# A second block of filter rows turned by DMA instead of TensorE, in a kernel whose order is a searched list

## The chip, the cores and the metric

The kernel runs on one core of one Trainium2 chip. The metric is the device time of one execution in microseconds (us). Three executions of the kernel before took 339.56, 339.56 and 339.36 us, median 339.56. A core has engines that run side by side, each one strictly through its own list of instructions: TensorE (PE, matrix multiplies into PSUM), VectorE (DVE), ScalarE (ACT), GpSimd (POOL) and SyncE (SP), whose list holds nearly all DMA issues. An engine stops at an instruction whose operand has not been signalled yet, and everything behind it in its list stops too.

## The reference, cut to what matters

Two kinds of layer alternate, twice each, on a sequence of 2048 rows of 512 columns in bfloat16:

```
def A(q, k, v, shift_k, ssm_k, ssm_D):            # long convolution
    kv = (4-tap causal filter of k along the rows, one tap set per column) * v
    y  = irfft(rfft(kv, 4096) * rfft(ssm_k, 4096))[:2048]     # along the rows, per column
    y  = y + kv * ssm_D
    return q * y
def B(x, w_gate, w_up, w_down):                   # gated MLP, 512 -> 1792 -> 512
    return (silu(x @ w_gate) * (x @ w_up)) @ w_down
x = A_q
x = x + A(layernorm(x), A_k, A_v, A_shift_k, A_ssm_k, A_ssm_D)
x = x + B(layernorm(x), B_w_gate, B_w_up, B_w_down)
(the same two lines once more)
```

In both A layers k, v, the taps and the filter are the same, so the convolution's result is computed once and used twice. The filter `ssm_k` is called h below; it lies in memory as 512 columns by 2048 rows, that is, turned against the layout in which the transform needs it.

## The kernel before, in words

**Blocks.** The 2048 rows are cut into four blocks of 512 rows. A block lies in SBUF as 128 partitions by four interleaved rows (`R = 4`) by 512 columns. The convolution works by blocks: `X[i]` is the spectrum of block i of kv, `H[b]` that of block b of h, `G[b]` joins `H[b]` and `H[b-1]`, and block k of the result is the inverse transform of the sum of `X[i]*G[j]` over i + j = k. The transforms are matmuls with tables of sines and cosines (`fwd`, `inv`) followed by additions on DVE. The MLP works on units of 256 rows (layer, block, half). For a unit, TensorE multiplies with `wg_sb` and `wu_sb` into PSUM (tile `pf`), ACT evicts both products, DVE multiplies them, and TensorE multiplies with `wd_sb` (tile `pd`). Some units take the down product by a seven-product scheme (`STRASSEN`, function `seven`), which needs sums of blocks of the down weights; `weight_sums` makes them once.

**How h is turned.** `load_h` (L428 and following, one DMA of 512 KB a block) brings block b into `hn` as columns by rows. `spectrum_h` then makes `hs`, rows by columns, in one of two ways, chosen by `H_DMA`. `transpose_h` uses TensorE: 16 transposes of 128x128 (L567) into two PSUM tiles, each evicted by one ACT copy of 128x1024 (L577). `transpose_h_dma` uses four ACT copies of 128x512 that put the rows apart (`hr`, L681) and then four SBUF-to-SBUF DMA transposes on SP's queue, one per interleaved row (L685). `forward4` follows in both cases: for each of the four rows of `hs`, two matmuls of 512 columns, each into a PSUM bank of its own that ACT evicts (L509). In the kernel before, blocks 0 and 1 of h are turned on TensorE and blocks 2 and 3 by DMA. Block 0's spectrum is evicted as the string `EVE` says, one letter for each of its eight banks (A for ACT L509, D for DVE L512).

**The order.** The program first records every operation in a `Plan`, with its engine, a cost that the author estimated, and its operands. The list `ORDER` holds one rank for each recorded operation; sorting by rank gives the order in which each engine's instructions are issued. `walk` lays the sorted operations on a time line by the estimated costs; that only decides which slot of a ring of buffers a tile takes and where idle matmuls (`wm`) warm TensorE at the start. So the order around the change is a fixed list; nothing is decided while the kernel runs.

**Rings.** A ring is a set of equal buffers: `s8` has eleven, `h`, `k`, `hs` have one each, `pf` (PSUM) four. An operation that writes a new tile into a ring waits until the readers of the tile that had the slot are done.

**The opening stage.** The first MLP unit cannot start before the first block of the convolution is done: spectra of block 0 of h and kv (L509, L548), their products on DVE (L732, L736), the inverse transform (L879), the layer norm (L898, L889, L950), and a transpose on TensorE (`ptz`, L1008) evicted into `zT` (L1011, L1013). TensorE fills the gaps of that chain with the convolution's block 1: turning h (L567), its forward matmuls (`ps<-hs,fwd`, L400), and the tap filter of k (`ps<-dg,kTb`, L400, 16 matmuls of 128 columns for each of four rows).

**SP's queue in the opening stage**, in its order: the loads of h, k, v, q, block 1 of h and v, the gate weights, two DMA transposes for `inv`, one for block 1 of k, the up weights, the down weights in two parts, block 1 of q, block 2 of h, block 2 of k.

Of the kernel before, what the change touches and what calls it, by code (L numbers as in the profile page):

```python
# [9 lines left out]
P = 128  # L10
# [9 lines left out]
H_DMA = lambda b: b in {2, 3}  # L20
# [13 lines left out]
LH0 = 4.0  # L34
# [7 lines left out]
EVE = "ADADAAAA"  # L42
# [80 lines left out]

PASSES, WARM, FETCH, PHASE, TOOK = 4, 33, 256, 173, 1.1

NS = 8
BLOCKS = [("C", 0, 1), ("C", 1, 1), ("C", 2, 1), ("C", 3, 1),
# [198 lines left out]
def kernel(  # L328
# [58 lines left out]
    def whole(name, shape, dtype=BF16, parts=1):  # L387
        return new("one", name, shape, dtype, parts)
# [631 lines left out]
    ws = {}  # L1020
# [498 lines left out]
```

## Time and profile before

| what | value |
|---|---|
| median of three runs | 339.56 us |
| the profiled execution, its own time | 340.1 us |
| its span (first to last instruction) | 338.3 us |
| PE busy | 333.9 us, 99% |
| DVE busy | 299.8 us, 89% |
| ACT busy | 265.0 us, 78% |
| POOL busy | 34.5 us, 10% |
| granted TensorE clock | 1.0 |

A row of a group reads: line, engine, operation, output and inputs, how many, then busy time and mean duration. Matmuls overlap in the pipeline, so the mean duration of one (379 ns for 512 columns) is longer than its step from one to the next; the chain that ended last gives the step. A row of SP's timeline is the time in which SP issues a transfer, not the time in which data move; the "to landing" rows count from the start of the issue until the transfer is signalled as done. A releaser is inferred from semaphores.

### The profile page before, as it was taken

What the parts mean: (1) busy time and instruction counts of PE and PEld (TensorE: products, weight loads), DVE (VectorE), ACT (ScalarE), POOL (GpSimd) and SP (SyncE); (2) the same over time, 40 slices, a digit from 0 to 9 for tenths busy, and PEclk for the clock granted to TensorE, in tenths of its full rate; (3) what the DMA queues carried; (4) which work ended last, traced back from release to release, by engine and by line L of the source; (5) the groups of instructions that cost most, each with busy time, mean ns of one, the idle gap of its engine ahead of it and who ended that gap; (6) DMA issues with size and microseconds to landing.
All of it is one profiled execution on the core that took longest, in us unless ns stands there. A gap on an engine that the chain in (4) does not pass through costs nothing.

```text
span 338.3 us, 5940 instructions
## 1 busy us (share of the span) xinstructions
PE 333.9 (99%) x2172; PEld 205.7 (61%) x2172; DVE 299.8 (89%) x508; ACT 265.0 (78%) x543; POOL 34.5 (10%) x48
## 2 busy tenths in 40 slices
PE   9999999999999999999999999999999999999996
PEld 8665865645454564745444564644546587867884
DVE  7899999999779997999999999989997967977465
ACT  6989999999987477989999886989765555566473
POOL 4010011003100000132030000101200010100000
PEclk9999999999999999999999999999999999999999
DMA  7999501443355336381333263510504230203201
GB/s 266 341 290 365 75 0 33 84 107 90 64 125 93 81 79 155 62 159 32 62 48 67 57 107 116 105 34 16 96 16 96 56 85 2 48 17 78 64 3 62
DMA packets 77992, 31.59 MB, mean 93 GB/s; under 512 B 69765, under 2 KB 75786, under 8 KB 77962
## 3 DMA queue, kind: packets, MB, share of 16 engines
q1 hardware_dynamic: 77808, 31.13, 39.8%
q8 instruction: 17, 0.28, 0.3%
q14 instruction: 13, 0.11, 0.1%
q10 hardware_dynamic: 154, 0.07, 0.1%
HBM read 12.33 MB, written 2.10 MB: 43 GB/s over the span
## 4 chain that ended last, share of the span: by engine, by line
PE 87%; ACT 7%; DVE 5%; issue 1%; POOL 0%; DVEq 0%; POOLq 0%
PE pf L400 50%; PE pd L1200 17%; PE ps L1075 7%; PE ps L400 7%; PE ps L548 2%; ACT jk L922 2%; PE wm L1485 1%; PE ps L879 1%; ACT sg L1113 1%; ACT hr L1114 1%; ACT X L509 1%; PE pt L567 1%; DVE t L746 1%; DVE m L630 1%; DVE Z L750 1%; DVE t L742 1%
## 5 line engine op out<-in xcount | busy, mean ns | idle before, releaser
L400 PEld LDWEIGHTS <-zT 128*128 128x128 bf16 x528 | 51.5, 98 | 59.4 <-DMA zT<-z 0.9
L400 PE MATMUL pf<-wu_sb,zT 128*128 128x512 bf16 x264 | 65.0, 379 | 0.0
L400 PE MATMUL pf<-wg_sb,zT 128*128 128x512 bf16 x264 | 64.9, 379 | 0.0
L1200 PE MATMUL pd<-wd_sb,sg 128*128 128x512 bf16 x200 | 49.4, 379 | 0.0
L1113 ACT ACTIVATE sg<-pf 128x512 bf16<-128x512 f32 x66 | 38.7, 604 | 11.4 <-PE pf L400 10.3
L400 PE MATMUL pf<-zT,wg_sb 128*128 128x256 bf16 x368 | 46.7, 273 | 0.0
L1114 ACT CAST hr<-pf 128x512 bf16<-128x512 f32 x66 | 38.2, 591 | 9.6 <-PE pf L400 9.0
L400 PE MATMUL pf<-zT,wu_sb 128*128 128x256 bf16 x368 | 45.4, 273 | 0.2 <-ACT zT L1013 0.2
L742 DVE TENSOR_TENSOR t<-X,G 128x4096 bf16<-128x4096 bf16 x18 | 41.0, 2280 | 0.1
L400 PEld LDWEIGHTS <-wg_sb 128*128 128x128 bf16 x368 | 36.0, 98 | 8.0
L400 PEld LDWEIGHTS <-wu_sb 128*128 128x128 bf16 x368 | 36.0, 98 | 7.1 <-issue 0.5
L1173 ACT ACTIVATE sg<-pf 128x512 bf16<-128x512 f32 x46 | 27.5, 606 | 10.9 <-PE pf L400 9.7
L1177 ACT CAST ht<-pf 128x512 bf16<-128x512 f32 x46 | 27.3, 599 | 10.8 <-PE pf L400 10.4
L889 POOL TENSOR_TENSOR rstd<-mv,nhalf 128x2 f32<-128x2 f32 x20 | 18.5, 928 | 160.3 <-DVE mv L899 160.3
L1200 PEld LDWEIGHTS <-sg 128*128 128x128 bf16 x200 | 19.6, 98 | 21.5
L1200 PE MATMUL pd<-wd_sb,ht 128*128 128x512 bf16 (+1 forms) x126 | 29.1, 369 | 0.0
L898 DVE BATCH_NORM_STATS2 bst<-xc 128x6 f32<-128x512 bf16 x40 | 26.4, 682 | 0.5
L1180 DVE TENSOR_TENSOR ht<-ht,sg 128x512 bf16<-128x512 bf16 (+1 forms) x31 | 16.7, 546 | 9.5 <-ACT sg L1173 6.2
L889 POOL TENSOR_TENSOR rstd<-ve,nhalf 128x2 f32<-128x2 f32 x12 | 12.4, 1032 | 112.3 <-ACT ve L926 112.3
L1120 DVE TENSOR_TENSOR hr<-hr,sg 128x1024 bf16<-128x1024 bf16 x27 | 18.4, 681 | 4.3 <-ACT hr L1114 2.3
L509 ACT ACTIVATE X<-ps 128x512 bf16<-128x512 f32 x32 | 18.8, 611 | 2.2 <-DVE Z L746 1.1
L1200 PEld LDWEIGHTS <-ht 128*128 128x128 bf16 x126 | 12.3, 98 | 12.8 <-ACT z L945 0.3
(143 smaller groups left out, 525.7 us busy)
## 6 DMA issues: line engine op xcount, KB each, us to landing
hn<-in_A_ssm_k_dram SPq DMA_DIRECT2D x4, 512.0 KB, 4.0
vt<-in_A_v_dram SPq DMA_DIRECT2D x4, 512.0 KB, 6.0
xc<-in_A_q_dram SPq DMA_DIRECT2D x4, 512.0 KB, 5.3
out_dram<-xc SPq DMA_DIRECT2D x15, 128.0 KB, 1.8
wg_sb<-in_B_w_gate_dram SPq DMA_DIRECT2D x1, 1792.0 KB
wu_sb<-in_B_w_up_dram SPq DMA_DIRECT2D x1, 1792.0 KB, 7.9
wd_sb<-in_B_w_down_dram SPq DMA_DIRECT2D x1, 1280.0 KB, 13.2
sg<-hr SPq DMA_TRANSPOSE x66, 2.4
```

The lines of the kernel that those rows point to most:

```text
L400: nc.tensor.matmul(o, lhsT=lhsT, rhs=rhs, start=(n == 0), stop=(n == len(terms) - 1))
L509: add("ACT", act(D), lambda: nc.scalar.activation(out=view(), in_=ps.t[:], func=ACT.Copy, scale=scale), r=[ps], w=[(buf, keys)], conv=conv)
L742: dve(8 * D, lambda t=t, part=part: nc.vector.tensor_mul(out=t.t[:], in0=x.t[:, :, part:part + 1, :].to_broadcast((P, R, 2, D)), in1=g.t[: ...
L889: add("POOL", cost, lambda: nc.gpsimd.tensor_tensor(out=rstd.t[:], in0=var(), in1=nhalf.t[:].to_broadcast((P, n)), op=ALU.pow), r=reads + ...
L898: add("DVE", 0.6, lambda st=st, i=i: nc.vector.bn_stats(out=st.t[:, 0:6], in_=xs[c].t[:, i, :]), r=[(xs[c], (i,))], w=[st])
L1075: nc.tensor.matmul(bank.t[:, half_ * C:(half_ + 1) * C], lhsT=lhsT(i), rhs=rhs(i), start=(first and i == 0 and half_ == 0), stop=(last and ...
L1113: add("ACT", act(D), lambda ps=ps, dst=dst, o=o, which=which: nc.scalar.activation(out=rows(dst, o), in_=ps.t[:], func=ACT.Silu) if which ...
L1114: out=rows(dst, o), in_=ps.t[:], func=ACT.Silu) if which == "g" else nc.scalar.copy(out=rows(dst, o), in_=ps.t[:]),
L1120: dve(n * W, lambda: nc.vector.tensor_mul(out=hr.t[:], in0=hr.t[:], in1=sg.t[:]), [sg], [hr], due=(unit, k / pairs, 0.0, "h"))
L1173: add("ACT", act(D), lambda ps=ps, o=o, sg=sg: nc.scalar.activation(out=sg.t[:, o:o + 2, :], in_=ps.t[:], func=ACT.Silu), r=[ps], w=[(sg, ...
L1177: add("ACT", act(D), lambda ps=ps, o=o, ht=ht: nc.scalar.copy(out=ht.t[:, o:o + 2, :], in_=ps.t[:]), r=[ps], w=[(ht, (o // 2,))], due=(uni ...
L1200: nc.tensor.matmul((pds[o] if not cs.start else pds[HP]).t[:, cs], lhsT=ht.tiles(q, o), rhs=wt["d"].t[:, ft, cs], start=(ft == std0 and no ...
```

## The change

Five edits:

1. `H_DMA` takes block 1 in: its h is turned by `transpose_h_dma` too.
2. The second letter of `EVE` goes from D to A: one eviction of block 0's spectrum of h moves from DVE (L512) to ACT (L509).
3. `weight_sums` writes five tiles of one size into the rings `h`, `k`, `hs`, `dg` and `s8`, where it wrote three tiles into `s8`; the diagonal tap tables `dg` get a ring of their own, so that their buffer can be used again. `seven` reads the tiles under the new names. Two of the five additions take even and odd rows of the weights instead of the lower and upper half.
4. Two numbers of the planner change: the estimated landing of block 0's h (`LH0`, 4.0 to 3.85), and a longer cost of TensorE's operations in the first 5.4 us (`RAMP`).
5. `ORDER` is another list, with 1725 ranks where there were 1721 (four operations fewer on TensorE and ACT, eight more on ACT and SP).

```
-H_DMA = lambda b: b in {2, 3}
+H_DMA = lambda b: b in {1, 2, 3}
...
-LH0 = 4.0
+LH0 = 3.85
...
-EVE = "ADADAAAA"
+EVE = "AAADAAAA"
...
 ORDER = [
-    1, 64, 179, 187, 2, 5, 0, 11, 15, 3, 4, 8, 14, 34, 36, 9, 7, 10, 6, 13, 19, 18, 17, 16, 20, 25, 27, 45, 51, 41, 47, 48, 31, 55, 33, 42, 32, 39,
...
+    4, 29, 43, 46, 3, 6, 5, 14, 21, 2, 11, 0, 36, 37, 38, 8, 9, 7, 10, 12, 22, 13, 16, 19, 20, 31, 33, 32, 44, 39, 52, 54, 28, 41, 27, 50, 30, 61, 40,
...
-PASSES, WARM, FETCH, PHASE, TOOK = 4, 33, 256, 173, 1.1
+PASSES, WARM, FETCH, PHASE, TOOK, RAMP = 4, 33, 256, 173, 1.1, 5.4
...
             o.end = o.start + o.cost
+            if o.eng == "PE" and o.start < RAMP:
+                o.end += 0.48 * min(1.92 * o.cost, RAMP - o.start)
...
-    dg = whole("dg", [P, KD, KS, P], parts=KD * KS)
+    dg = new("dg", "dg", [P, KD, KS, P], parts=KD * KS)
...
-        a = ws["14"] = new("s8", "wsa", [P, 2, NF // 2, C], parts=2)
-        b = ws["3"] = new("s8", "wsb", [P, NF // 2, C])
-        c = ws["67"] = new("s8", "wsc", [P, NF, C])
...
+        a0, a1 = (new(ring, "wsa", [P, NF // 2, C]) for ring in ("h", "k"))
+        b = new("hs", "wsb", [P, NF // 2, C])
+        c0, c1 = (new(ring, "wsc", [P, NF // 2, C]) for ring in ("dg", "s8"))
+        ws.update({"1": a0, "4": a1, "3": b, "6": c0, "7": c1})
+        for out, x0, x1, op in ((a0, lambda: ev(lo), lambda: od(hi), ALU.add), (b, lambda: ev(hi), lambda: od(hi), ALU.subtract),
+                                (a1, lambda: od(lo), lambda: ev(lo), ALU.subtract), (c0, lambda: ev(lo), lambda: ev(hi), ALU.add),
+                                (c1, lambda: od(lo), lambda: od(hi), ALU.add)):
+            dve(NF // 2 * C, lambda out=out, x0=x0, x1=x1, op=op: nc.vector.tensor_tensor(out=out.t[:], in0=x0(), in1=x1(), op=op),
+                [wd], [out])
```

What the new list does to the opening stage is read from the instruction lists of the two kernels. SP's queue, from the tap-filtered block 1 of k on:

```
before                              after
block 1 of k, transposed            block 1 of k, transposed
up weights                          hs<-hr, rows 1 to 3 (three transposes)
down weights, first 4 of 14 rows    up weights
down weights, other 10 rows         hs<-hr, fourth row
block 1 of q                        down weights, other 10 rows
block 2 of h                        block 1 of q
block 2 of k, transposed            block 2 of h
                                    down weights, first 4 of 14 rows
                                    block 2 of k, transposed
```

TensorE's list of the changed kernel between the last spectrum matmul of block 0's kv and the first MLP matmul (`xN` is N matmuls; the weight loads of the forward matmuls wait for the transfer named):

```
ps<-vt,fwd 512 columns x32         (block 0's kv, with nothing between them)
ps<-hs,fwd 512 x1                  waits for the first turned row
ps<-dg,kTb 128 x16                 waits for block 1 of k
ps<-hs,fwd 512 x2                  waits for the second turned row
ps<-dg,kTb 128 x16
ps<-hs,fwd 512 x2                  waits for the third turned row
ps<-m,inv 512 x13
ps<-hs,fwd 512 x1
ps<-m,inv 512 x3
ps<-hs,fwd 512 x1                  waits for the fourth turned row
ps<-dg,kTb 128 x16
ps<-hs,fwd 512 x1
ps<-dg,kTb 128 x16
ptz<-ident,z 128 x8
ps<-vt,fwd 512 x2
pf<-zT,wg_sb 256 x8 ...            (first MLP unit)
```

ACT's list has the four `hr` copies of block 1 among the last evictions of block 0's spectra: two before the last `ev`, one after it, and the fourth after three of the eight `X` evictions. ACT's evictions of the two forward banks of the fourth row stand before the two last `ks` evictions of the tap filter and the `zT` copy.

More of the change, by code (lines that the diff above doesn't have):

```diff
@@ L374, in span @@
         return slice(rows[0], rows[-1] + 1, rows[1] - rows[0])
-    plan = Plan({"h": 1, "k": 1, "v": 1, "hs": 1, "x": 2, "y": 2, "s8":11, "n": 2, "jk": 1, "dn": 1, "ks": 2, "z": 3, "zT":3,
+    plan = Plan({"h": 1, "k": 1, "v": 1, "hs": 1, "dg": 1, "x": 2, "y": 2, "s8":11, "n": 2, "jk": 1, "dn": 1, "ks": 2, "z": 3, "zT":3,
                  "ht":7, "st": 4, "bn": BN_SLOTS, "mv": 9, "ve": 8, "rs": 6, "pf": 4, "pc": 2, "pd": 2, **RINGS})
@@ L1027, in weight_sums @@
         lo, hi = slice(0, C), slice(C, D)
-        a = ws["14"] = new("s8", "wsa", [P, 2, NF // 2, C], parts=2)
-        b = ws["3"] = new("s8", "wsb", [P, NF // 2, C])
-        c = ws["67"] = new("s8", "wsc", [P, NF, C])
-        for out, keys, x0, x1, op in (
-                (lambda: a.t[:, 0], [(a, (0,))], lambda: ev(lo), lambda: od(hi), ALU.add),
-                (lambda: b.t[:], [b], lambda: ev(hi), lambda: od(hi), ALU.subtract),
-                (lambda: a.t[:, 1], [(a, (1,))], lambda: od(lo), lambda: ev(lo), ALU.subtract)):
-            dve(NF // 2 * C, lambda out=out, x0=x0, x1=x1, op=op: nc.vector.tensor_tensor(out=out(), in0=x0(), in1=x1(), op=op),
-                [wd], keys)
-        for n in range(2):
-            sl = slice(n * NF // 2, (n + 1) * NF // 2)
-            dve(NF // 2 * C, lambda sl=sl: nc.vector.tensor_tensor(out=c.t[:, sl], in0=wd.t[:, sl, lo], in1=wd.t[:, sl, hi], op=ALU.add),
-                [wd], [c])
+        a0, a1 = (new(ring, "wsa", [P, NF // 2, C]) for ring in ("h", "k"))
[7 more added lines that the diff above has]
+                [wd], [out])
     def strided(src, off, dims):
@@ L1060, in seven @@
         for bank, rd, terms in (
-                (e, [ht, ws["14"], ws["3"]], (
-                    (0, lambda i: ht.tiles(2 * i + 1, 1), lambda i: ws["14"].t[:, 1, f0 + i]),
+                (e, [ht, ws["4"], ws["3"]], (
+                    (0, lambda i: ht.tiles(2 * i + 1, 1), lambda i: ws["4"].t[:, f0 + i]),
                     (1, lambda i: ht.tiles(2 * i, 0), lambda i: ws["3"].t[:, f0 + i]))),
@@ L1066, in seven @@
                     (1, lambda i: cb.t[:, 1, i], lambda i: wd.t[:, 2 * (f0 + i), 0:C]))),
-                (r, [(cb, (1,)), ws["67"]], (
-                    (0, lambda i: cb.t[:, 3, i], lambda i: ws["67"].t[:, 2 * (f0 + i) + 1]),
-                    (1, lambda i: cb.t[:, 2, i], lambda i: ws["67"].t[:, 2 * (f0 + i)]))),
-                (o, [(cb, (2,)), ws["14"]], (
-                    (0, lambda i: cb.t[:, 4, i], lambda i: ws["14"].t[:, 0, f0 + i]),))):
+                (r, [(cb, (1,)), ws["6"], ws["7"]], (
+                    (0, lambda i: cb.t[:, 3, i], lambda i: ws["7"].t[:, f0 + i]),
+                    (1, lambda i: cb.t[:, 2, i], lambda i: ws["6"].t[:, f0 + i]))),
+                (o, [(cb, (2,)), ws["1"]], (
+                    (0, lambda i: cb.t[:, 4, i], lambda i: ws["1"].t[:, f0 + i]),))):
             def go(bank=bank, terms=terms):
```

126 rows, old and new, of the table ORDER are left out of this document.

## The prediction

> **What bounds the kernel now.** I read the page's first part, then the waits of TensorE, then the chain that ended last.
>
> ```profile
> PE 333.9 (99%) x2172; PEld 205.7 (61%) x2172; DVE 299.8 (89%) x508; ACT 265.0 (78%) x543; POOL 34.5 (10%) x48
> ```
>
> ```profile
> PE wm L1485 <- PEq L1503: 0.8, 1, 0.8
> PE ptz L1008 <- DVE z L950: 0.3, 1, 0.3
> PE pf L400 <- ACT zT L1013: 0.2, 1, 0.2
> ```
>
> TensorE is busy 99% of the span, and it waits three times in all, for 1.3 us together. Only work taken off TensorE, or a wait given to it, can move the end. The chain gives its steps and the places in the opening stage:
>
> ```profile
> 0.77 2.40 PE wm L1485 x21
> 3.39 1.39 PE wm L1485 x12
> ...
> 14.71 5.18 PE ps L548 x24
> 19.89 0.45 PE pt L567 x8
> ...
> 22.29 0.45 PE pt L567 x8
> ...
> 24.27 0.89 PE ps L400 x16
> ...
> 33.22 5.40 PE pf L400 x48
> ...
> 316.29 6.99 PE pf L400 x64
> ...
> 333.96 1.32 PE pd L1200 x12
> ```
>
> A matmul of 512 columns steps at 5.18/24 = 0.216 us, one of 256 at 6.99/64 = 0.109, sixteen of 128 take 0.89. The first MLP unit starts at 33.22 and the last matmul ends at 335.28, so 302.1 us lie between. The work of that stretch, counted from the instruction list, is 904 matmuls of 512 columns and 973 of 256: 904 x 0.2158 + 973 x 0.1092 = 301.3. From 33.22 on a better order can recover 0.8 us at most. So the time is when the first MLP unit starts, plus a constant, and the opening stage decides.
>
> **The change part by part.**
>
> *TensorE.* It loses the 16 transposes of block 1 of h: the two `pt L567 x8` rows above, 2 x 0.45 = 0.90 us, all ahead of 33.22 and all on TensorE's list. That is -0.90 if everything else keeps up.
>
> *ACT and DVE.* Rows of the tiles and of the opening stage:
>
> ```profile
> L681 ACT COPY hr<-hn x4: 652/659/687, 51.1 to 58.1; 128x512 bf16<-128x512 bf16 x4
> ...
> L577 ACT COPY hs<-pt x4: 586/802/1021, 5.2 to 23.9; 128x512 bf16<-128x512 bf16 x2, 128x1024 bf16<-128x1024 bf16 x2
> L509 ACT ACTIVATE ev<-ps x6: 591/598/615, 8.7 to 14.8; 128x512 bf16<-128x512 f32 x6
> L512 DVE TENSOR_SCALAR ev<-ps x2: 683/688/692, 9.0 to 10.2; 128x512 bf16<-128x512 f32 x2
> ...
> 18.21 0.60 ACT L509 ACTIVATE X<-ps 128x512 bf16<-128x512 f32 x1 [0.27 <-PE ps L548]
> 19.50 1.09 ACT L509 ACTIVATE X<-ps 128x512 bf16<-128x512 f32 x2 [0.70 <-PE ps L548]
> ...
> 24.99 1.90 DVE L873 TENSOR_TENSOR m<-Z 128x1024 bf16<-128x1024 bf16 x3
> ```
>
> ACT gains four copies of 0.66 and one eviction of 0.60 and loses two evictions of 1.02: 4 x 0.66 + 0.60 - 2 x 1.02 = +1.2 us. It waited 0.27 + 0.70 us for TensorE in that stretch, which covers most of it; I cost the rest at nothing because the four PSUM banks of `pf` let TensorE run ahead. Without that cover the last `X` evictions would come up to 1.2 us later. DVE loses one eviction of 0.69, so its last `m` ends near 26.3 instead of 26.9, and the chain to the layer norm gains up to 0.6. That matches the 0.90 of TensorE: both halves of the opening shrink together, and without a new wait the first unit would start near 32.4.
>
> *SP's queue.* Here is the step that I think decides.
>
> ```profile
> 3.75 0.43 SPq L487 DMA_DIRECT2D wg_sb<-in_B_w_gate_dram  x1
> 4.73 11.60 SPq L1372 DMA_TRANSPOSE inv<-fwd  x2
> 16.38 2.61 SPq L444 DMA_TRANSPOSE kTb<-in_A_k_dram  x1
> 19.04 0.58 SPq L487 DMA_DIRECT2D wu_sb<-in_B_w_up_dram  x1
> ...
> 70.93 2.56 SPq L685 DMA_TRANSPOSE hs<-hr  x2
> ```
>
> The rows up to block 1 of k stay as they are, so the first turned row is issued at 19.0. Each issue takes 2.56/2 = 1.28. Three rows go out by 22.9, the up weights go out at 22.9 instead of 19.04, and the fourth row is issued at about 23.5, behind 1792 KB of weights in the same queue. What a transfer takes from issue to signal:
>
> ```profile
> wu_sb<-in_B_w_up_dram SPq DMA_DIRECT2D x1, 1792.0 KB, 7.9
> hs<-hr SPq DMA_TRANSPOSE x8, 2.5
> inv<-fwd SPq DMA_TRANSPOSE x2, 13.2
> ```
>
> Undisturbed, a row takes 2.5, and the first three land near 21.5, 22.8 and 24.1. Transposes behind a load of 512 KB are seen twice later in the run. First `xc` at 129.83, which landed after 3.8, and the second of three `hs` rows, issued at 131.5, which landed after 3.3:
>
> ```profile
> 129.83 0.34 SPq L476 DMA_DIRECT2D xc<-in_A_q_dram  x1
> 130.22 3.85 SPq L685 DMA_TRANSPOSE hs<-hr  x3
> ```
>
> ```profile
> DMA to landing us min/median/max: 3.8/3.8/3.8
> ```
>
> ```profile
> DMA to landing us min/median/max: 3.3/3.3/3.3
> ```
>
> The load was done at 133.6 and the row at 134.8, 1.1 later. Then `vt`, and a transpose issued 0.62 behind it, with its landing, and what a load of that size takes in a quiet stretch:
>
> ```profile
> 144.75 0.54 SPq L472 DMA_DIRECT2D vt<-in_A_v_dram  x1
> 145.37 1.19 SPq L980 DMA_TRANSPOSE zT<-z  x1
> ```
>
> ```profile
> DMA to landing us min/median/max: 5.5/5.5/5.5
> ```
>
> ```profile
> vt<-in_A_v_dram SPq DMA_DIRECT2D x1, 512.0 KB, 3.7
> ```
>
> This one took 5.5 instead of 2.5 and was done at 150.9; `vt` by its usual 3.7 at 148.4, so 2.4 earlier. The `inv` row says the same: a transpose issued 1.0 us after the gate weights took 13.2.
>
> When does the fourth row land? The up weights went out while block 1 of k was still moving, and took 7.9. In a quiet queue I estimate 3.7 for the first 512 KB and 1280 KB more at the 365 GB/s of the page's fourth slice:
>
> ```profile
> GB/s 266 341 290 365 75 0 33 84 107 90 64 125 93 81 79 155 62 159 32 62 48 67 57 107 116 105 34 16 96 16 96 56 85 2 48 17 78 64 3 62
> ```
>
> 1.31 MB / 0.365 = 3.6, so 7.3. The weights then land between 22.9 + 7.3 = 30.2 and 30.8, and the row 0 to 2.4 us later, 30.2 to 33.2. I take 30.2 + 1.1 = 31.3, by the `hs` case, the same transfer. Not held at all, it would land at 23.5 + 2.5 = 26.0.
>
> The Trainium skill, "DMA: Bandwidth & Descriptors", section on queues, rings and completion order, says that descriptors on one engine are consumed in ring order, and that a transfer's signal is a write that lands only after every earlier write from that engine. By that rule alone the row is signalled with the weights and no later, 30.2 to 30.8, and the sum below would be +0.6 to +1.2 instead of +1.7. The rows above agree in kind and say more.
>
> When does TensorE want it? By the list of the changed kernel: 32 matmuls from 14.71 (32 x 0.216 = 6.9) end at 21.6; five forward matmuls and two tap groups (5 x 0.216 + 2 x 0.89) end at 24.5; sixteen inverse matmuls and one forward (17 x 0.216) end at 28.2. The first three rows, and block 1 of k, come within some tenths of their turn. The fourth is wanted at 28.2 and lands at 31.3: a wait of 3.1 us, on an engine that had waited 1.3 in all. Behind it in TensorE's list stand the rest of the tap filter, `ptz` and the whole first unit, which cannot pass. DVE has its `z` ready by then and waits too.
>
> After the landing TensorE needs two forward matmuls and two tap groups, 2 x 0.216 + 2 x 0.89 = 2.2 us, and then what it took before from `ptz` to the first unit:
>
> ```profile
> 31.78 0.72 PE L1008 MATMUL ptz<-ident,z 128*128 128x128 bf16 x8 [0.31 <-DVE z L950]
> 33.22 1.03 PE L400 MATMUL pf<-zT,wu_sb 128*128 128x256 bf16 x8 [0.17 <-ACT zT L1013]
> ```
>
> 33.22 - 31.78 = 1.44. So the unit starts 3.65 us after the landing, 31.3 + 3.65 = 34.95, against 33.22: **+1.7 us**. It breaks even at a landing of 29.6.
>
> *Down weights.* With the up weights 3.9 later and the first part last, that part lands near 40 (2.75 MB at the rate of the stretch after the fourth row). The first `pd` matmul comes 96 x 0.109 = 10.5 us after the first unit starts, at 45; nothing waits. If the unit did start at 32.4, the need at 43 still leaves 3 us.
>
> *Weight sums.* One group of them:
>
> ```profile
> L1035 DVE TENSOR_TENSOR wsa<-wd_sb x2: 1084/1084/1085, 222.3 to 224.0; 128x1792 bf16<-128x1792 bf16 x2
> ```
>
> Five additions of one size before and after, on DVE late in the run; the moved buffers free `s8` slots. I cost them at nothing: DVE is off TensorE's path there. If that cover were gone, their place could cost a step of 1.1 us.
>
> *The rest of the new list.* It can give back 0.8 at most, as worked out above, and can lose more where a new order meets a late operand; I take 0, between -0.8 and +1.
>
> Sum: -0.90 (transposes) is already inside the start of the unit; +1.7 stands for the opening as a whole, 0 for the rest. The profiled execution took 340.1, 0.54 above the median; I apply the difference to the median: 339.56 + 1.7 = **341.3 us**, +0.5%.
>
> **The rivals.**
>
> *The row is not held (faster).* If the fourth transpose overtakes the weights and lands before 28.2, TensorE never waits for it, the first unit starts near 32.4, and the transposes' 0.90 is the whole effect: 339.56 - 0.90 = 338.7 us. For it: a transpose needs no bandwidth of HBM, and the list puts its first use 5 us behind its issue, twice the undisturbed 2.5. Against it: the 3.3, 5.5 and 13.2 rows. The point that decides is a landing of 29.6.
>
> *Held, but short (same).* A landing between 28.9 and 30.3 ends within 0.2% of before, 339.6. It takes up weights that land in 6 to 7 us instead of 7.3 to 7.9, with the row close behind.
>
> *The wait cools TensorE (slower still).* The first 33 matmuls of 128 columns ran at 2.40/21 = 0.114 and 1.39/12 = 0.116 us, against 0.45/8 = 0.056 later, from 0.77 to 4.78. If a wait of 3 us or more brought that rate back for as long again, half of the 4.0 us would be lost on top: 343.3. Against it: no wait in this trace is long enough to tell. In a sentence of the Trainium skill ("TensorE: Matmul & The Clock Gate", Part 1) an idle window of about 3.4 us halves the clock; a 3.1 us wait would just miss it, and no row here shows it.
>
> **How the numbers follow.** A difference of 0.2% (0.7 us) is about what a measurement of this kernel can tell from none. Chances: held as forecast 0.62, held and cooled 0.08, short 0.06, not held 0.24. That gives faster 0.24, same 0.06, slower 0.70. The forecast's own range is a landing of 30.2 to 33.2, with a rest of 0: 340.2 to 343.1. The range that holds 8 in 10 reaches to most of the faster case and part of the cooled one: 338.2 to 343.4.
>
> **What would show it.** Right: TensorE's waits have a new row on the forward matmul of the turned rows (L402 in the changed kernel), released by a DMA, 2 to 5 us, near 28; the first `pf` matmul starts near 35; the stretch from there to the last matmul stays 302 us. Wrong: the first `pf` matmul before 33.2 and no such row; or that stretch longer than 303, which would put the cause in the rest of the list. If the first `hs` row comes late because ACT's copies end after 19, everything behind it on SP moves too, and the loss is larger than forecast.

## The result: 1.2% slower, and the profile after

| | before | after |
|---|---|---|
| median of six runs each | 339.62 us | 343.89 us |
| ratio, 95% interval | | 1.0117 [1.0099, 1.0136] |
| the profiled execution, its own time and span | 340.1, 338.3 us | 343.91, 342.0 us |
| first `pf` matmul starts | 33.22 us | 35.90 us |
| from there to the end of the last matmul | 302.06 us | 303.04 us |
| granted TensorE clock | 1.0 | 1.0 |

The forecast was 341.3 us, with a range up to 343.4. The sign and the wait for the fourth row are as forecast; the time lies above the range. The two profiled executions differ by 3.7 us of span, and the table splits them: 2.68 before the first MLP unit and 0.98 behind it.

First part 1 of the page of the changed kernel, then its waits of TensorE (line waited for: us in total, times, longest).

```profile
PE 332.6 (97%) x2156; PEld 204.2 (60%) x2156; DVE 300.3 (88%) x507; ACT 265.8 (78%) x546; POOL 39.1 (11%) x48
```

```profile
PE ps L402 <- DMA hs<-hr: 2.9, 2, 1.8
PE ps L881 <- ACT H L511: 1.3, 1, 1.3
PE pf L402 <- ACT hr L1112: 1.0, 1, 1.0
PE wm L1483 <- PEq L1501: 0.8, 1, 0.8
PE ps L402 <- DVE vt L607: 0.3, 1, 0.3
```

TensorE lost the 16 transposes and 1.3 us of busy time, and it now waits 6.3 us, where it waited 1.3. The largest row is the one that the prediction named, but it holds two waits: 1.77 for the fourth turned row, and 1.12 for the first, which landed near 22.2 and not 21.5 and which the prediction had within some tenths of its turn. The next two rows, 1.3 and 1.0, it did not have. The chain that ended last, in the opening stage (start, us, what), and the landing of the load ahead:

```profile
22.94 0.59 SPq L489
23.53 0.05 issue
23.58 8.64 DMA hs<-hr
32.22 0.05 issue
32.26 1.51 PE ps L402 x18
```

```profile
wu_sb<-in_B_w_up_dram SPq DMA_DIRECT2D x1, 1792.0 KB, 8.7
```

The up weights are issued at 22.94 and land 8.7 later, at 31.6; the fourth turned row, issued 0.64 behind them, lands at 32.22, 0.6 after them. TensorE's timeline of the changed kernel has the waits, the first unit and the late wait:

```profile
22.29 0.39 PE L402 MATMUL ps<-hs,fwd 128*128 128x512 bf16 x1 [1.12 <-DMA hs<-hr]
...
28.61 1.02 PE L881 MATMUL ps<-m,inv 128*128 128x512 bf16 x4 [1.33 <-ACT H L511]
...
32.26 0.39 PE L402 MATMUL ps<-hs,fwd 128*128 128x512 bf16 x1 [1.77 <-DMA hs<-hr]
...
35.90 1.03 PE L402 MATMUL pf<-zT,wg_sb 128*128 128x256 bf16 x8
...
249.93 2.32 PE L402 MATMUL pf<-wu_sb,zT 128*128 128x512 bf16 x10 [0.97 <-ACT hr L1112]
```

The wait of 1.33 near 28 and that of 0.97 near 249 have the same origin, two operands back: GpSimd's `rstd`, one power of 128x2 numbers. Its rows in both kernels, then what VectorE did meanwhile and what ScalarE waited for it in the changed one:

```profile
17.35 1.17 POOL L889 TENSOR_TENSOR rstd<-ve,nhalf 128x2 f32<-128x2 f32 x1 [11.06 <-ACT ve L926]
```

```profile
22.98 3.92 POOL L891 TENSOR_TENSOR rstd<-ve,nhalf 128x2 f32<-128x2 f32 x1 [16.19 <-ACT ve L928]
...
245.94 2.30 POOL L891 TENSOR_TENSOR rstd<-ve,nhalf 128x2 f32<-128x2 f32 x1 [3.02 <-ACT ve L928]
```

```profile
22.82 1.09 DVE L738 TENSOR_TENSOR Z<-t,t 128x512 bf16<-128x512 bf16 x3
23.82 2.50 DVE L875 TENSOR_TENSOR m<-Z 128x1024 bf16<-128x1024 bf16 x4
28.10 0.69 DVE L992 TENSOR_TENSOR n<-n,ps 128x512 bf16<-128x512 bf16 x1 [1.78 <-ACT n L947]
...
245.33 2.36 DVE L748 TENSOR_TENSOR t<-t,t 128x2048 bf16<-128x2048 bf16 x2
247.72 2.29 DVE L752 TENSOR_TENSOR Z<-Z,t 128x4096 bf16<-128x4096 bf16 x1
```

```profile
26.93 0.29 ACT L940 ACTIVATE nmr<-nm,rstd 128x1 f32<-128x1 f32 x1 [2.24 <-POOL rstd L891]
...
248.27 0.29 ACT L940 ACTIVATE nmr<-nm,rstd 128x1 f32<-128x1 f32 x1 [1.99 <-POOL rstd L891]
```

The same instruction takes 1.17 us before in the opening, and 3.92 there and 2.30 near 246 after; GpSimd's busy time rose from 34.5 to 39.1. (Long ones of 2.77 and 2.57 stand in the kernel before too, near 148 and 175, where TensorE does not wait.) It ends 0.58 after VectorE's run of `m` ends (23.82 + 2.50 = 26.32, `rstd` ends at 26.90), and 0.55 after the pair L748 (247.69, 248.24). Two more things had changed for the first of them. ScalarE's two squares and the sum that `rstd` needs stood early in the old order (`ve` at 16.97) and stand among the `X` evictions in the new one (`ve` at 22.60). And the new order's VectorE run has no break there: each operation begins before the one ahead of it has ended. So I read a second wait behind the first: without the fourth row's, the unit would not have started at 32.4, as the prediction had it for a row that is not held. The experiments test that.

### The profile page after: what moved, and what is told of

It is laid out like the page before. It is cut to its first block, busy times and chain, and to the rows that moved or that the text cites. A ratio compares the mean times of both kernels' runs of the same rounds, so it can differ in the third digit from the quotient of the medians.

```text
span 342.0 us, 5910 instructions
## 1 busy us (share of the span) xinstructions
PE 332.6 (97%) x2156; PEld 204.2 (60%) x2156; DVE 300.3 (88%) x507; ACT 265.8 (78%) x546; POOL 39.1 (11%) x48
## 3 DMA queue, kind: packets, MB, share of 16 engines
q1 hardware_dynamic: 79984, 31.66, 39.1%
## 4 chain that ended last, share of the span: by engine, by line
PE 86%; ACT 6%; DMA 3%; SPq 1%; DVE 1%; issue 1%; ACTq 0%
PE pf L402 52%; PE pd L1198 18%; PE ps L1073 7%; PE ps L402 6%; DMA hs<-hr 3%; ACT hr L1112 1%; PE wm L1483 1%; ACT jk L924 1%; SPq L687 1%; PE ps L550 1%; ACT sg L1111 1%; DMA sg<-hr 1%; DVE t L744 1%; ACT jk L915 1%; ACT X L511 0%
## 5 line engine op out<-in xcount | busy, mean ns | idle before, releaser
L402 PEld LDWEIGHTS <-zT 128*128 128x128 bf16 x528 | 51.5, 98 | 59.8 <-issue 1.3
L402 PE MATMUL pf<-wu_sb,zT 128*128 128x512 bf16 x264 | 65.0, 379 | 1.0 <-ACT hr L1112 1.0
L402 PE MATMUL pf<-wg_sb,zT 128*128 128x512 bf16 x264 | 65.2, 379 | 0.1
L1111 ACT ACTIVATE sg<-pf 128x512 bf16<-128x512 f32 x66 | 39.3, 606 | 10.9 <-PE pf L402 8.3
L402 PE MATMUL pf<-zT,wu_sb 128*128 128x256 bf16 x368 | 46.4, 273 | 0.0
L402 PE MATMUL pf<-zT,wg_sb 128*128 128x256 bf16 x368 | 46.2, 273 | 0.0
L402 PEld LDWEIGHTS <-wu_sb 128*128 128x128 bf16 x368 | 36.0, 98 | 8.0
L402 PEld LDWEIGHTS <-wg_sb 128*128 128x128 bf16 x368 | 36.0, 98 | 7.7 <-DVE zT L1013 0.2
L1171 ACT ACTIVATE sg<-pf 128x512 bf16<-128x512 f32 x46 | 27.7, 613 | 9.9 <-PE pf L402 7.6
L891 POOL TENSOR_TENSOR rstd<-mv,nhalf 128x2 f32<-128x2 f32 x20 | 17.5, 873 | 139.9 <-DVE mv L901 139.9
L891 POOL TENSOR_TENSOR rstd<-ve,nhalf 128x2 f32<-128x2 f32 x12 | 17.7, 1478 | 128.7 <-ACT ve L928 128.7
```

The source lines that it names most:

```text
L402: nc.tensor.matmul(o, lhsT=lhsT, rhs=rhs, start=(n == 0), stop=(n == len(terms) - 1))
L891: add("POOL", cost, lambda: nc.gpsimd.tensor_tensor(out=rstd.t[:], in0=var(), in1=nhalf.t[:].to_broadcast((P, n)), op=ALU.pow), r=reads + ...
L1111: add("ACT", act(D), lambda ps=ps, dst=dst, o=o, which=which: nc.scalar.activation(out=rows(dst, o), in_=ps.t[:], func=ACT.Silu) if which ...
L1171: add("ACT", act(D), lambda ps=ps, o=o, sg=sg: nc.scalar.activation(out=sg.t[:, o:o + 2, :], in_=ps.t[:], func=ACT.Silu), r=[ps], w=[(sg, ...
```

## The experiments

Two theories. **T1**: the fourth row's wait is all that moved the first unit. **T2**: there are two waits, stacked; the late `rstd` is the second, and a third `rstd` causes the 1.0 us near 249. All kernels below are the changed kernel with ranks of `ORDER` replaced (`n: rank`, n counts the recorded operations), unless said otherwise; three lines are added ahead of the rest, so L402 of the changed kernel is L405 in most of them. The kernel before ran beside each.

| kernel | median, us | ratio to before | first `pf` | from there to the last matmul |
|---|---|---|---|---|
| before (profiled) | 339.62 | | 33.22 | 302.06 |
| changed | 343.89 | 1.0117 [1.0099, 1.0136] | 35.90 | 303.04 |
| fourth row ahead of the weights | 343.05 | 1.0104 [1.0089, 1.0120] | 35.02 | 303.12 |
| statistics early | 343.79 | 1.0133 [1.0099, 1.0168] | 34.66 | 303.11 |
| both | 342.42 | 1.0090 [1.0075, 1.0105] | 34.97 | 303.22 |
| fourth row later | 349.13 | 1.0283 [1.0266, 1.0300] | 42.37 | 303.29 |
| late `nmr` on VectorE | 342.90 | 1.0138 [1.0073, 1.0203] | 35.56 | 302.40 |
| that, early `nmr` too, row first | 340.90 | 1.0042 [1.0027, 1.0058] | 33.62 | 302.69 |
| early and late `nmr`, row behind the weights | 344.21 | 1.0152 [1.0129, 1.0176] | 37.06 | 302.46 |
| that, weights in two halves | 340.70 | 1.0044 [1.0030, 1.0058] | 33.50 | 302.29 |
| turn on TensorE, new order | 344.25 | 1.0138 [1.0122, 1.0155] | 35.47 | 303.35 |
| before, one eviction moved | 339.53 | 1.0003 [0.9992, 1.0013] | 32.77 | 302.01 |
| before, `ve` late | 343.52 | 1.0121 [1.0106, 1.0136] | 36.77 | 301.91 |

The last two columns come from one profiled execution of each kernel, which is not the median: it took 343.09 us for "both", 350.56 for "fourth row later" and 341.19 for the early and late `nmr` with the row first (the slowest of four each time), and 342.68 for "statistics early" (the fastest). The ratio of "late `nmr` on VectorE" is pulled up by one execution of 346.91; its other three took 342.58 to 342.93.

### The fourth row ahead of the weights

```
ORDER.update({169: 204.5})          # 169: fourth turned row; the up weights are at 205
```

> Edit: on SP's queue the fourth turned row of the second block's h is issued ahead of the 1792 KB up weights; all else as in the changed kernel. Theory T1 (that row's wait is all that moved the first unit's start): the row lands with its three sisters near 22 to 26 us, the 1.8 us wait near 32 goes, the first up matmul starts at 33.2 or before, time 340.3 to 341.2. Theory T2 (behind that wait stands a second one, the late rstd of GpSimd): the first up matmul starts near 35.1, time near 343.1. Rival R (the row is late of itself, whatever stands ahead of it): it lands after 30, time 343.9.

The unit started at 35.02 and the time was 343.05: T2, within 0.1 of its numbers. The row's wait is gone, and the chain that ended last now runs through GpSimd:

```profile
22.59 0.30 ACT ve L931
22.89 0.07 issue
22.96 3.93 POOL rstd L894
26.89 0.02 issue
26.92 0.30 ACT nmr L943
```

### Statistics early, and both

```
ORDER.update({165: 115.1, 104: 115.2, 106: 115.4, 105: 123.2, 107: 123.4})   # one hr copy, nm, two squares, ve
```

> Edit: the first block's layer-norm squares and its sum of squares stand earlier on ScalarE, ahead of the residual's evictions, as does one of the four h copies; the queue of SP is that of the changed kernel. GpSimd's rstd should start near 19 us and not at 23, and take about 1.2 us and not 3.9. T1 and T2 (the fourth row's landing at 32.2 sets the start): the first up matmul stays at 35.9, time 343.9. Theory T3 (the late rstd alone sets it, the row's wait would be hidden without it): at least 1 us faster, time 342.9 or less.

> Edit: both of the former two together. T2 (two waits, one behind the other): the first up matmul starts at 32.9 to 33.3, as before or a little earlier; the 1.0 us wait of TensorE near 249 us stays, so time 340.5 to 341.2. T1: no faster than with the fourth row moved alone.

Moved early, `rstd` took 0.72 us and was done at 20.1. That did not bring what T2 had promised: both edits together gave 342.42, and a start at 34.97, not 33, in an execution of 343.09. ScalarE has no slack in that stretch. What is put ahead of the `X` evictions makes VectorE wait for them, and its run of `m` ends 2.3 us later than in the changed kernel. VectorE's timeline with both edits:

```profile
17.79 1.29 DVE L737 TENSOR_TENSOR t<-X,G 128x1024 bf16<-128x1024 bf16 x2 [1.27 <-ACT X L514]
19.85 0.69 DVE L737 TENSOR_TENSOR t<-X,G 128x1024 bf16<-128x1024 bf16 x1 [0.77 <-ACT X L514]
...
26.15 2.49 DVE L878 TENSOR_TENSOR m<-Z 128x1024 bf16<-128x1024 bf16 x4
```

The median of the kernel with the early statistics alone, 343.79, is what both theories gave, but its profile tells little: in that execution, the fastest of four from 342.68 to 345.57, the up weights landed after 7.3 us, not 8.7, and the fourth row was there when TensorE wanted it at 30.94.

### The fourth row later

```
ORDER.update({81: 205.2})           # the ten-row part of the down weights, ahead of the row too
```

> Edit: the 560-KB-or-so second part of the down weights is put ahead of the fourth turned row too, behind the up weights, so that the row stands one load further back in SP's queue. If the row is held by what stands ahead of it in the queue, it lands about 3.5 us later (near 35.7), the first up matmul starts near 39.4 and the time is near 347.4. If the row is late for another reason (the amount of data under way in all, its own cost) the landing stays within 0.5 us of 32.2 and the time at 343.9.

(That part is 1280 KB; the expectation gives its size wrong.) The row landed at 36.6, 4.4 later than in the changed kernel and 0.9 later than forecast: it is held by what is issued ahead of it in the queue. The median rose by 5.2, and the profiled execution took 6.65 more than that of the changed kernel; both are more than the landing, and TensorE's rows show why. The first fence is its timeline; the second is a table by stretches (stretch, us, busy time and instructions of PE, PEld, DVE, ACT, POOL, then the granted clock).

```profile
36.62 0.61 PE L405 MATMUL ps<-hs,fwd 128*128 128x512 bf16 x1 [4.99 <-DMA hs<-hr]
37.02 1.91 PE L405 MATMUL ps<-dg,kTb 128*128 128x128 bf16 x16
```

```profile
36.00:40.00 4.00, 3.38 (x26) 2.83 (x27) 0.00 (x0) 1.20 (x3) 0.00 (x0) 0.50 1.05 353
```

After a wait of 4.99 us the clock was 0.50, and sixteen tap matmuls took 1.91 and not 1.06. In this execution it had fallen once already, behind the wait for the first row:

```profile
23.27 0.39 PE L405 MATMUL ps<-hs,fwd 128*128 128x512 bf16 x1 [2.20 <-DMA hs<-hr]
```

```profile
24.00:28.00 4.00, 4.00 (x31) 2.80 (x30) 2.21 (x4) 2.52 (x6) 2.79 (x1) 0.57 0.84 232
```

The unit started 5.75 after the landing, where the changed kernel needed 3.68.

### The small products on VectorE

`nmr = nm * rstd` (two products of 128x1) is made by ScalarE. On VectorE it makes VectorE wait for `rstd`, which gives GpSimd its break. For the late pair alone (these two operations only):

```
-                add("ACT", TINY, lambda o=o: nc.scalar.mul(out=nmr.t[:, o:o + 1], in_=mean.t[:, o:o + 1], mul=rstd.t[:, o:o + 1]),
+                add("DVE", 0.08, lambda o=o: nc.vector.tensor_tensor(out=nmr.t[:, o:o + 1], in0=mean.t[:, o:o + 1],
+                    in1=rstd.t[:, o:o + 1], op=ALU.mult),
...
+ORDER.update({1286: 1267.5, 1287: 1267.6, 1288: 1268.1})    # between the two halves of L748
```

> Edit: in the normalisation whose rstd ends late at 248.2 us, the two small products nmr = nm * rstd (128x1 each) are made on VectorE, between the two halves of its 2.36 us pair of operations, and not on ScalarE. VectorE then waits for rstd there, which leaves GpSimd a gap to run it in. Theory H (GpSimd's pow is held while VectorE works without a gap): rstd ends near 247.1 and not 248.2, ScalarE's n starts near 247.3 and not 248.6, TensorE's 0.97 us wait near 249 goes, and the stretch from the first up matmul to the last matmul falls from 303.05 back to about 302.1; time near 342.9. Rival L (the 1.0 us comes from something else in the new order): the wait or one like it stays, time 343.9.

`rstd` took 1.16 and not 2.30, TensorE ran on, and the stretch behind the first unit fell from 303.04 to 302.40: 0.6 of the 0.98 us. Its timelines of GpSimd and TensorE:

```profile
245.51 1.16 POOL L894 TENSOR_TENSOR rstd<-ve,nhalf 128x2 f32<-128x2 f32 x1 [3.02 <-ACT ve L931]
```

```profile
248.37 2.75 PE L405 MATMUL pf<-wu_sb,zT 128*128 128x512 bf16 x12
```

With the opening's pair too, and the fourth row first:

```
ORDER.update({169: 204.5, 109: 174, 110: 174.1, 1286: 1267.5, 1287: 1267.6, 1288: 1268.1})
```

> Edit: as in the kernel with the fourth turned row ahead of the up weights, and the nmr products of the first block's normalisation and of the late one on VectorE. Theory H: the first block's rstd ends near 24.1 and not 26.9, VectorE's n starts near 27.2 and not 28.1, the first up matmul near 34.1 and not 35.0, the late wait is gone; time near 341.1. Rival: rstd is not what holds the start; the first up matmul stays at 35.0 and only the late 1.0 us goes: 342.1.

340.90 us, with the unit at 33.62: 3.0 us of the 4.3 are gone, the theory's 341.1 within 0.2. GpSimd's and VectorE's rows:

```profile
23.11 1.18 POOL L894 TENSOR_TENSOR rstd<-ve,nhalf 128x2 f32<-128x2 f32 x1 [16.32 <-ACT ve L931]
```

```profile
24.32 0.23 DVE L944 TENSOR_TENSOR nmr<-nm,rstd 128x1 f32<-128x1 f32 x2 [0.61 <-POOL rstd L894]
...
27.21 0.68 DVE L998 TENSOR_TENSOR n<-n,ps 128x512 bf16<-128x512 bf16 x1
```

### Only the second wait taken away

The same without moving the fourth row.

> Edit: both pairs of nmr products (first block's and late one) on VectorE, the fourth turned row left behind the up weights. Theory S (two waits stacked in the opening, either of which alone holds the start near 35 to 36): GpSimd's rstd ends near 24.3, VectorE's z is ready near 32, but TensorE still waits for the fourth row, wanted now at 29.5, until it lands near 31.9; first up matmul at 35.6, time near 342.9, no better than with the late pair alone. Rival (the rstd was the whole of the later start): first up matmul at 34.1 or before, time 341.2 or less.

No better, as T2 said, but 1.3 above the 342.9 that it gave: 344.21. The row is there at 32.05, as in the changed kernel (32.22), but TensorE's idle time is now one piece of 2.89 us and not two, and the clock fell. TensorE's timeline of this kernel, the stretch behind the wait, and the same stretch of the changed kernel:

```profile
32.05 0.61 PE L405 MATMUL ps<-hs,fwd 128*128 128x512 bf16 x1 [2.89 <-DMA hs<-hr]
32.45 1.91 PE L405 MATMUL ps<-dg,kTb 128*128 128x128 bf16 x16
```

```profile
32.00:36.00 4.00, 3.95 (x39) 3.40 (x40) 0.11 (x2) 1.74 (x4) 0.00 (x0) 0.61 1.09 356
```

```profile
32.00:36.00 4.00, 3.45 (x45) 2.77 (x46) 2.94 (x9) 3.29 (x8) 0.69 (x1) 1.00 1.10 355
```

The unit starts 5.01 us after the landing instead of 3.68, 1.3 us more.

### The weights in two halves

On top of the kernel just described, the up weights are loaded as 896 KB ahead of the fourth row and 896 KB behind it.

```
+    up = B_w_up.rearrange("(k p) f -> p k f", p=P)
...
-        nc.sync.dma_start(out=wt[which].t[:], in_=src)
+        nc.sync.dma_start(out=wt[which].t[:, 0:2], in_=src[:, 0:2])      # for the up weights
+        nc.sync.dma_start(out=wt["u"].t[:, 2:], in_=up[:, 2:])           # issued ahead of the ten rows of down weights
```

> Edit: as nmr_both, and the up weights are loaded in two halves of 896 KB, one ahead of the fourth turned row and one behind it. From the two landings measured with 1792 KB (8.64 us after its issue) and with 1792 + 1280 KB (11.7 us) ahead of it, 2.4 us per 1000 KB: the row should land 6.5 us after its issue, near 30.0, TensorE waits 0.5 us for it (wanted at 29.5), first up matmul near 33.8, time near 341.1. If the hold does not go by the bytes ahead of the row in the queue: landing stays at 31.9, time 342.9.

SP's timeline, the landings of the two halves, and TensorE's first use of the row:

```profile
23.30 0.59 SPq L497 DMA_DIRECT2D wu_sb<-in_B_w_up_dram  x1
23.94 1.19 SPq L695 DMA_TRANSPOSE hs<-hr  x1
```

```profile
DMA to landing us min/median/max: 5.9/7.1/8.3
```

```profile
29.81 0.39 PE L405 MATMUL ps<-hs,fwd 128*128 128x512 bf16 x1 [0.18 <-DMA hs<-hr]
```

The first half landed at 29.2, the row 0.6 after it at 29.8, 5.9 after its issue (expected 6.5), and the time was 340.70: the hold goes by the bytes ahead. (TensorE's other wait for a turned row in this kernel, 1.6 us, is for the first one.)

### The turn on TensorE in the new order

```
-H_DMA = lambda b: b in {1, 2, 3}
+H_DMA = lambda b: b in {2, 3}
+ORDER = ORDER[:165] + [142.5, 156.5, 132.5, 137.5] + ORDER[173:]     # two groups of transposes, two evictions
```

> Edit: part 1 alone undone in the new order: the second block's h is turned on TensorE again (two groups of eight transposes, two 1.02 us evictions on ScalarE, between the residual's evictions), the four ScalarE copies and four turned rows on SP's queue go. Theory Q (turned rows and their copies are the cause of the later start): TensorE's two waits for turned rows go, the first up matmul at 33.2 to 33.6, and with the late 1.0 us the time is 340.4 to 340.8. Theory O (the new order is the cause, through VectorE's run without a gap and GpSimd's late rstd): the first up matmul stays near 35.0, time 342.6 to 343.1.

344.25 us. No wait for a turned row is left, and the unit starts at 35.47 all the same, through the late `rstd`:

```profile
24.14 3.20 POOL L892 TENSOR_TENSOR rstd<-ve,nhalf 128x2 f32<-128x2 f32 x1 [17.15 <-ACT ve L929]
```

So the second wait does not need the DMA turn; the new order brings it without. It is not a clean undoing: where I put the two evictions, they delay `ve` to 23.76, 1.2 later than in the changed kernel, so its size is not to be read from this run.

### One eviction alone, and `ve` late in the old order

```
-EVE = "ADADAAAA"                   # in the kernel before
+EVE = "AAADAAAA"
```

> Edit: the kernel before with one change only, the eviction of the second part of the first block's h forward product (the third letter of EVE) on ScalarE and not VectorE, in the old order. Costed at nothing in the prediction: time within 0.2% of before. If that eviction is what makes ScalarE too full in the opening: at least 0.7 us slower.

339.53 against 339.36 us beside it, ratio 1.0003 [0.9992, 1.0013]: that edit costs nothing. (It is the second letter of `EVE`; the expectation says third.)

```
ORDER.update({105: 156.1, 106: 156.2, 107: 156.3, 108: 156.4})     # in the kernel before: squares, ve, rstd
```

> Edit: the kernel before, with one thing moved: the two squares of the first block's layer norm and its ve stand behind the eight evictions of the residual on ScalarE, as in the changed kernel; nothing else of the change is in it. Theory H (GpSimd's pow, issued into VectorE's run without a gap, ends 0.6 us behind that run): rstd starts near 22.2 and ends between 25.5 and 27.4, ScalarE's n starts near 27.6 and not 24.8, the first up matmul starts near 34.7 and not 33.2, time 340.4 to 341.0. Rival: the pow takes its 1.2 us there too, n starts near 24.8 and the time stays within 0.2% of before.

Neither theory's numbers. The time rose by 4.2 us, but `rstd` was not held. Rows of GpSimd, VectorE and TensorE:

```profile
24.42 0.82 POOL L892 TENSOR_TENSOR rstd<-ve,nhalf 128x2 f32<-128x2 f32 x1 [18.04 <-ACT ve L929]
```

```profile
23.23 1.43 DVE L739 TENSOR_TENSOR Z<-t,t 128x512 bf16<-128x512 bf16 x4
24.69 1.90 DVE L876 TENSOR_TENSOR m<-Z 128x1024 bf16<-128x1024 bf16 x3
```

```profile
26.10 0.38 PE L882 MATMUL ps<-m,inv 128*128 128x512 bf16 x1 [2.35 <-ACT H L512]
```

The old order has a break in VectorE's run: `Z` ends at 24.66 and `m` starts at 24.69. `rstd` ended at 25.24, 0.58 after the break began. The time went elsewhere: in ScalarE's list the squares, `ve` and the first `nmr` now stand ahead of evictions that TensorE needs, TensorE waited 2.35 us, and the clock fell to 0.84 and 0.73 in the two stretches of 4 us from 24.0 on. The run shows how little of a break GpSimd needs, and that late statistics cost 4 us in the old order by another way; it is no proof of the hold.

## Why the prediction was right in kind and wrong in size

*What bounds the kernel: right.* The time is when the first unit starts plus a stretch that hardly moves: over all thirteen profiles the start ranges from 32.8 to 42.4 us and the stretch from 301.9 to 303.4.

*TensorE's -0.90, the eviction, the weights' lateness: right.* The busy time fell by 1.3 us. One eviction alone measured nothing. No down product waited for its weights. The weight sums and the planner's numbers (edits 3 and 4) were not tested by themselves.

*The fourth row: right in mechanism, the size off.* This is the first step of the sum that failed. "30.2 + 1.1 = 31.3": the row landed at 32.22. The up weights took 8.7 and not 7.3 to 7.9; the row came 0.6 behind them, not 1.1. From the landing to the unit the forecast had 3.65 and the trace has 3.68. This term is 0.9 short. The prediction's "wanted at 28.2" was wrong as well: after the waits of 1.12 and 1.33 TensorE came to the row at 30.5, so that it waited 1.77 for it and not 3.1; the start goes by the landing and did not change by that. The landing of the same load varies between the kernels with the same queue: 7.3, 8.4, 8.6 and 8.7; what makes it vary stays open. The Trainium skill ("DMA: Bandwidth & Descriptors", on queues, rings and completion order) has the signal land after every earlier write of its engine. The landings agree: 5.9, 8.6 and 11.6 us after the row's issue with 896, 1792 and 3072 KB ahead of it, and 2.4 to 3.5 for turned rows with no such load ahead. The prediction's "with the weights and no later" does not hold: the row came 0.6 behind the weights.

*"I cost the rest at nothing" (ScalarE's 1.2 us): the reason was wrong, and the changed kernel hides it.* I compared ScalarE's work by sums and did not ask where its layer-norm squares had gone. In the old order both squares ran before the `X` evictions; in the new one the four copies and five `X` evictions stand ahead of the first square, and all eight ahead of the second. The statistics slid to 22.6, and GpSimd's power was issued into VectorE's run. This did not add to the changed kernel's start, because the fourth row came later still: its landing and the 2.2 us of matmuls behind it reach 34.4, `z` was ready at 34.0. But it set what was left when the row was on time: 35.02, and with that not the 32.4 of the rival "not held". That rival's 338.7 us would thus have been missed in this order even with a row that is not held. How much of the slide the copies force, and how much the searched list merely chose, the runs do not separate: with the statistics put early again, VectorE's run ended 2.3 us later.

*"I take 0, between -0.8 and +1" (the rest of the new list): the size off.* This is the second step of the sum that failed. The rest measured +0.98, at the far end; the stretch of 303.04 just passes the 303 that the prediction had named as a sign of a cause in the rest of the list. About 0.6 of it is the `rstd` near 246, which went with the late pair on VectorE; the other 0.2 to 0.6 of the kernels without that wait stays unexplained.

*"The wait cools TensorE": the mechanism is real, not in this kernel.* The changed kernel's two idle pieces (1.33 and 1.77) left the clock at 1.00. One piece of 2.89 brought it to 0.61 in the stretch behind and cost 1.3 us.

The sum with the two terms as measured: 341.3 + 0.95 (start of the unit) + 0.98 (rest) = 343.2. Most of the remaining 0.7 is that the profiled execution of before lay 0.5 above its median, while that of after lay on its own.

What stays open: with both waits and the late one gone, the best kernel still takes 340.70 against 339.37, 0.4% more. Its unit starts at 33.50, against 32.77 in the profiled execution of the kernel with one eviction moved, whose 339.59 us is near the median of before; in the best kernel ScalarE's `ve` is still late (22.7) and makes VectorE wait 0.61. None of the versions beats the kernel before. Why the search put the row there can be read from the code but was not tested: `walk` counts a long load on SP's queue as 4.0 us and lets a turned row land 0.6 after that, 22.94 + 4.6 = 27.5, ahead of its use; it landed at 32.22. Likewise `walk` lets GpSimd's power wait for the end of one VectorE operation at most (`settle`), never for a run of them; this too is read from the code.

## What to carry to other kernels

When a change moves work to an engine, follow the small operations that were in its way, not the sum of its time: here the sum was 1.2 us, but in the new order a statistic stood 5.6 us later, and that decided what the queue's wait hid. Where two waits stand one behind the other, taking one away shows little or makes it worse; take away both before judging either. Put a transfer that someone waits for ahead of a long load in the same queue, or cut the load: here the row followed the load by 0.6 us, with 896 KB as with 1792.

## What the runs showed of the hardware

- A GpSimd instruction of 0.7 to 1.2 us (`rstd`, 128x2) took 3.92 us while VectorE worked without a break on operations with two inputs in SBUF, seven in a row, and 2.30 us near 246. In these places it ended 0.55 to 0.58 us after the first break, and breaks of 0.03 us were enough (247.69 to 247.72 there, 24.66 to 24.69 in "before, `ve` late"). Given a break by a VectorE operation that waited for it, it took 1.16 to 1.18. Not every such run holds it: in the changed kernel the `rstd` that starts at 61.53 ended at 63.27, 0.55 after one VectorE operation ended (62.72), though the next (`hr`, 62.64 to 63.32) had begun before that. What makes the difference stays open. The Trainium skill ("SBUF — State Buffer", section "SBUF: two separate sides") calls the port pair that the two engines share an exclusive lock for a whole instruction, and the loser blocks; the trace agrees, and shows the loser blocked over a run of instructions in two places.
- TensorE's granted clock fell around single waits of 2.20, 2.35, 2.89 and 4.99 us (to 0.57, 0.73, 0.61 and 0.50 in a stretch of 4 us behind them), and stayed at 1.00 after 1.77. The Trainium skill ("TensorE: Matmul & The Clock Gate", Part 1) gives an idle window of about 3.4 us; here 2.20 was enough, so the measurement decides, and the prediction's "a 3.1 us wait would just miss it" was wrong. Each of these is one execution; whether the length of the wait alone decides was not tested.
